# Clustered attention and two gated layers on one core: pair loads behind the mask rows, one set's mask transposed in one go each way, one scratch tile in SBUF

## The chip, the cores and the metric

One program on one core of one Trainium2 chip. The time is device microseconds (us) of one execution, lower is better. Engines: TensorE (PE; its weight loads are PEld), VectorE (DVE), ScalarE (ACT), GpSimd (POOL) and SyncE (SP), which issues nearly all transfers.

## What is computed

From the reference, cut to what matters here:

```python
q_assign = np.argmax(np.einsum('bhsd,hcd->bhsc', q_n, c_n), axis=-1)      # q, k: (2, 8, 768, 64); 16 clusters a head
k_assign = np.argmax(np.einsum('bhsd,hcd->bhsc', k_n, c_n), axis=-1)
mask = q_assign[:, :, :, None] == k_assign[:, :, None, :]
scores = np.where(mask, scale * np.matmul(q, k.transpose(0, 1, 3, 2)), -1000000000.0)
attn = softmax(scores); x = np.matmul(attn, v)                            # then (1536, 512)
h = x @ w_in                                                              # first layer, d_ff 2048
g = (a[0] + a[1] * h + a[2] * h**2 + a[3] * h**3) / (1.0 + np.abs(b[0]) * np.abs(h) + np.abs(b[1]) * h**2 + 1e-06)
x = g @ w_out
# second layer, d_ff 1024: x @ w_in, h * softmax(h), normalised, @ w_out
```

A query attends to the keys of its own cluster only.

## The kernel before

The attention runs over 16 heads of 6 units each (a unit is 128 queries of a head; `units`, index `idx` = 6 n + t for head n and unit t). `unit_scores` makes the scores of a unit in PSUM from four operands: `q1`, `k1` (L398) and `q2`, `k2` (L404). `unit_max` takes the row extreme on DVE (L409), `unit_exp` the exponential on ACT (L422), `turn_p` transposes two units' weights on DVE (L442), and `pv_step` multiplies with the values on PE (L454), one or two heads behind. There are two sets of the four operands, for even and odd heads (`NB = 2`).

The mask sits in 16 extra rows, 64 to 79, of `q2` and `k2`: one row a cluster. They are made for several heads at once. A set (`sets`) is two to four pair tiles `pr` (128 x 768, the q or the k of two heads). Set 0 serves heads 0 and 1, set 1 heads 2 and 3, sets 2, 3 and 4 four heads each. From the pairs PE makes the similarities with the cluster centres (`sims`, L271); ACT copies them out (`keep`, L280); then, for set 1, PE transposes them by token (`by_token`, L284), DVE finds the first maximum (L291 to L305), PE transposes the result back (`mask_t`, L308) and ACT writes it as mask rows `oh1` (`mask_out`, L332). `set1_a` and `set1_b` do this for set 1 in two halves of three tiles each; their PSUM tile is the one that the value products `pv` use afterwards. From `oh` the rows are copied into `q2` and `k2` by two small transfers a head (L374 and L375, 48 KB each), at the end of `prep_head`, which on POOL makes the rest of the next head's operands from the tiles `dup` (loaded by `load_head`, L205 and L206).

All these loads go through SP's one queue, in the order in which they stand there. A tile scheduler fixes that order when the program is built. It hands each transfer the next of eight completion semaphores (`DMAHW0` to `DMAHW7`), so a transfer is issued only after the one eight places ahead of it has landed. The pairs of set k are loaded at unit `AT[k] - LD`, which is unit 17 for set 3 and unit 40 for set 4:

```python
AT = (0, 0, 8, 27, 50)
for k in range(3, len(sets)):
    if idx == AT[k] - LD:
        load_pairs(sets[k])
```

The first layer runs over 48 units too (`ff_units`, a block of 512 tokens by 128 of d_ff). Each has 12 matmuls `h` (L741), a gate on ACT, POOL and DVE (`ff_g1`, `ff_g2`, `ff_g3`, L809 to L831) and 12 matmuls `y` (L848). The gate takes a reciprocal as exp(-ln) and one Newton step; its scratch `r` is the unit's own PSUM tile `hp`. Units 0 and 1 share one PSUM tile of two banks, `h01`. ACT copies the last head's value products out as `u7` and `w7` (L470) behind the first gate's last operation.

Of the kernel before, what the change touches and what calls it, by code (L numbers as in the profile page):

```python
# [7 lines left out]
F32 = mybir.dt.float32  # L8
F32R = mybir.dt.float32r
BF16 = mybir.dt.bfloat16  # L10
# [7 lines left out]
NT = S // 128  # L18
# [12 lines left out]
def fused_kernel(ctx: ExitStack, tc: tile.TileContext, qT, kT, v, cent, w1, w2i, w2o, gln, coef, centT, cst, out):  # L31
    nc = tc.nc
# [17 lines left out]
    def psum4(name):  # L50

        return pvp[0].tile([128, 4, 512], F32, name=name, tag="pv", bufs=1)

    def bank(tag, name):
        return stp.tile([128, 512], F32, name=name, tag=tag)
# [129 lines left out]
    last = {}  # L185

    def load_pairs(es, parts=1):
        for pp, i in es:
            b, p = divmod(pp, 4)
            t = asp.tile([128, S], F32, name=f"pr{pp}{i}", tag="pr", bufs=4)  # L190
            raw["p", pp, i] = t
        w = S // parts
        for c in range(parts):
            for pp, i in es:
                b, p = divmod(pp, 4)
                nc.sync.dma_start(
                    out=raw["p", pp, i][:, w * c:w * c + w],
                    in_=(qT, kT)[i][b, 2 * p:2 * p + 2].rearrange("j d t -> (j d) t")[:, w * c:w * c + w])

    def load_head(n):  # L200
        b, h = divmod(n, H)
        for i, src in enumerate((qT, kT)):
            t = qk.tile([128, S], F32, name=f"dup{n}{i}", tag=f"dup{i}", bufs=2)
            if n:
                nc.sync.dma_start(out=t[0:64], in_=src[b, h])  # L205
            nc.sync.dma_start(out=t[64:128], in_=src[b, h])  # L206
            raw["d", n, i] = t
# [10 lines left out]
    sets = [[(0, 0), (0, 1)], [(1, 0), (1, 1)], [(2, 0), (3, 0), (2, 1), (3, 1)], [(4, 0), (5, 0), (4, 1), (5, 1)], [(6, 0), (7, 0), (6, 1), (7, 1)]]  # L218
# [7 lines left out]
    t = bank("a0", "warm")  # L226
# [22 lines left out]
    mk = {}  # L249
    MS, E, OH = {}, {}, {}  # L250
# [31 lines left out]
    def by_token(k, t, o):  # L282
        M = 32 * len(sets[k])
        return nc.tensor.transpose(o, E[k][0][0:M, t * 128:(t + 1) * 128], ident[0:M, 0:M])  # L284

    def is_max(k, t0, nt, o):
        g = 2 * len(sets[k])
        sv = o.rearrange("p t (g c) -> p t g c", c=C)
        ev = E[k][1][:, t0:t0 + nt].rearrange("p t (g c) -> p t g c", c=C)
        mx = sm.tile([128, nt, g], F32, name=f"mx{k}{t0}", tag=f"mx{nt}{g}", bufs=2)  # L290
        nc.vector.tensor_reduce(mx, sv, axis=AX.X, op=ALU.max)  # L291
        nc.vector.tensor_tensor(ev, sv, mx[:, :, :, None].to_broadcast([128, nt, g, C]), op=ALU.is_equal)

    def rank(k, eng):
        g = 2 * len(sets[k]) * NT
        ev = E[k][1].rearrange("p t (g c) -> p (t g) c", c=C)
        eng.tensor_tensor(ev, ev, rev[:, None, :].to_broadcast([128, g, C]), op=ALU.mult)
# [9 lines left out]
    def mask_t(k, t, o):  # L307
        return nc.tensor.transpose(o, E[k][2][:, t], identb)  # L308
# [20 lines left out]
    def mask_out(k, o, t):  # L329
        masked[k] += o.shape[-1] * (o.shape[1] if len(o.shape) > 2 else 1)  # L330
        M = t.shape[0]
        nc.scalar.activation(out=o, in_=t, func=AF.Identity, scale=MS[k][0:M, 0:1], bias=MS[k][0:M, 1:2])  # L332
# [4 lines left out]
    q2, k1, k2 = [None] * NB, [None] * NB, [None] * NB  # L337
# [8 lines left out]
    def rnd(eng, o, a, scale=1.0):  # L346
        if eng is nc.scalar:
            eng.activation(out=o, in_=a, func=AF.Copy, scale=scale)
            return
        if eng is nc.gpsimd:  # L350
            eng.tensor_scalar(o, a, scale, 0.0, op0=ALU.mult, op1=ALU.add)
        elif isinstance(scale, float) and scale == 1.0:
            eng.tensor_copy(o, a)
        else:
            eng.tensor_scalar(o, a, scale, None, op0=ALU.mult)

    def prep_head(n, er=None, es=None):
        er = er or nc.gpsimd
        es = es or nc.gpsimd
        b, h = divmod(n, H)  # L360
        i = n % NB
        a, c = raw.pop(("d", n, 0)), raw.pop(("d", n, 1))
        rnd(er, k1[i], c, sgn[:, 1:2])
        yield
        es.tensor_tensor(k2[i][0:64], c[0:64], k1[i][0:64].bitcast(F32), op=ALU.subtract)
        yield
        rnd(er, q1[i], a, sgn[:, 0:1])
        rnd(er, q2[i][0:64], a[0:64], -0.125)
        yield
        es.tensor_tensor(q1[i][64:128], a[64:128], q1[i][64:128].bitcast(F32), op=ALU.subtract)  # L370
        yield
        if n:
            assert masked[next(k for k, es in enumerate(sets) if (n // 2, 0) in es)] == S
            nc.sync.dma_start(out=q2[i][64:80].bitcast(F32), in_=mk.pop((n, 0)).bitcast(F32))  # L374
            nc.sync.dma_start(out=k2[i][64:80].bitcast(F32), in_=mk.pop((n, 1)).bitcast(F32))  # L375
        yield


# [201 lines left out]
    M = 32 * len(sets[0])  # L580
# [40 lines left out]
    mp1 = [None]  # L621
# [10 lines left out]

    def set1_a():
        mp1[0] = psum4("set1")
        for a in range(2):
            tp = mp1[0][:, a, 0:3 * M].rearrange("p (t m) -> p t m", t=3)
            for t in range(3):
                by_token(1, 3 * a + t, tp[:, t])
            is_max(1, 3 * a, 3, tp)
        rank(1, nc.vector)  # L640
        first_max(1)

    def set1_b():
        for a in range(2):
            tp = mp1[0][:, 2 + a].bitcast(BF16)
            for t in range(3):
                mask_t(1, 3 * a + t, tp[0:M, t * 128:t * 128 + 128])
            mask_out(1, OH[1][0:M, 384 * a:384 * a + 384], tp[0:M, 0:384])
    load_head(1)
    load_head(2)  # L650
    load_pairs(sets[2])
# [26 lines left out]
    for idx, (n, t) in enumerate(units):  # L678
        if idx == ACL:
            asg.close()  # L680
            wh["r"] = ctx.enter_context(tc.tile_pool(name="wh2", bufs=4, side="right"))
        for k in range(3, len(sets)):
            if idx == AT[k] - LD:
                load_pairs(sets[k])
        if t == 3 and 0 < n < B * H - 2:
            load_head(n + 2)
        if t == 0:
            if n >= 1 and n + 1 < B * H:
                spread(prep_head(n + 1), 7, idx, idx + 6)
        if t == 3:  # L690
            load_v(n)
        sp = unit_scores(n, t)
        m = unit_max(n, t, sp)
        if n == B * H - 1 and t >= NT - 2:
            if t == NT - 2:
                for _ in turn_p(n, NT // 2 - 2):
                    pass
            else:
                end = turn_p(n, NT // 2 - 1)
                next(end)  # L700
        elif t % 2 and idx > 1:
            for _ in turn_p(*divmod(idx // 2 - 1, NT // 2)):
                pass
        if idx == 2:
            with tc.issue_after(last["dve"].ins):
                set1_a()
        if idx == S1B:
            set1_b()
        if idx == 8:
            with tc.issue_after(last["act"].ins):  # L710
                nc.scalar.activation(out=ab, in_=coef_t[:, 4:6], func=AF.Abs)

        m_, i0, i1 = pv_part(n, t)
        if m_ >= 0:
            for i in range(i0, i1):
                pv_step(m_, i)
        if t == 0 and n and n % 2 == 0:
            sums_out(n // 2 - 1, pair_sums(n // 2 - 1), idx + 2)
        unit_exp(n, t, sp, m)
        if n >= 2 and t in (1, 2):  # L720
            pv_out(n - 2, t - 1)
            if t == 2 and n % 2:

                fin_ = pair_fin(n // 2 - 1)
                for i in (1, 2, 3, 4):
                    plan[min(96, idx + i)].append(fin_)
        run_plan(idx)
        if idx == 1:
            set1_0()
# [72 lines left out]
    live = {}  # L802

    def T(tag, u, dt=F32, bufs=1):
        return tmp.tile([128, 512], dt, name=f"{tag}{u}", tag=tag, bufs=bufs)

    def ff_g1(u, hp):
        t, q, y = T("t", u), T("q", u, bufs=2), T("y", u, bufs=3)
        nc.scalar.activation(out=t, in_=hp, func=AF.Abs)  # L809
        last["g"] = nc.scalar.activation(out=y, in_=hp, func=AF.Identity, scale=a3, bias=a2)  # L810
        nc.gpsimd.tensor_scalar(q, t, ab[:, 1:2], ab[:, 0:1], op0=ALU.mult, op1=ALU.add)  # L811
        nc.gpsimd.tensor_tensor(q, q, t, op=ALU.mult)  # L812
        nc.vector.tensor_tensor(y, y, hp, op=ALU.mult)  # L813
        nc.vector.scalar_tensor_tensor(y, y, a1, hp, op0=ALU.add, op1=ALU.mult)
        live[u] = (q, y, hp)

    def ff_g2(u):

# [196 lines left out]
    for u in range(NU + LAG):  # L1015
        if 1 <= u <= NU:
            ff_g2(u - 1)
        if u < NU:
            hp = ff_h(u)
# [77 lines left out]
```

## Time and profile before

| | us |
|---|---|
| median of 3 runs | 661.67 |
| the three runs | 660.16, 661.67, 663.62 |
| the profiled execution: its time | 663.3 |
| its span, first to last instruction | 661.4 |
| PE busy | 602.7 (91%) |
| DVE busy | 493.9 (75%) |
| ACT busy | 443.2 (67%) |
| POOL busy | 386.6 (58%) |

Times in rows are us from the start of the span. A row of an engine's timeline gives start, duration, engine, line, operation and, in brackets, how long the engine was idle before it and what ended that. The busy shares are means over stages with different limits: attention to about 240 us, the first layer to about 500 us, the second layer after it.

### The profile page before, as it was taken

Reading aid. Unit: us, or ns where it says so; the run is one execution under the profiler, and the core shown is the slowest. Engines: PE = TensorE matmul, PEld = TensorE weight load, DVE = VectorE, ACT = ScalarE, POOL = GpSimd, SP = SyncE. Lnnn points to the kernel's source line nnn. Section 1 sums busy time; section 2 is a strip of 40 time slices with the busy share of each in tenths; the row PEclk is TensorE's granted clock in tenths of the full one; section 3 lists DMA queues with packets and bytes.
Section 4 is the critical chain, followed back from the end, with each engine's and each line's share of the span. In section 5 each row is a group of like instructions: output and inputs, shape, how many; then the busy total and the mean of one; then the engine's idle time right before and its main releaser. Section 6 shows DMA issues by size and latency. Waiting matters only on the chain.

```text
span 661.4 us, 13794 instructions
## 1 busy us (share of the span) xinstructions
PE 602.7 (91%) x5517; PEld 469.9 (71%) x5517; DVE 493.9 (75%) x646; ACT 443.2 (67%) x807; POOL 386.6 (58%) x355
## 2 busy tenths in 40 slices
PE   5666897797788889999999999999999999999998
PEld 3444665565556567888888888887788888888887
DVE  4765989989999877897988977779799545444350
ACT  3543676776777778988989879799887434444251
POOL 7741868578679647988998988688977000000000
PEclk8887898999999999999999999999999999999999
DMA  9993558767585242321221322232100000000001
GB/s 214 229 245 100 133 138 238 197 183 190 159 215 134 79 142 94 99 94 63 96 96 64 101 62 92 64 97 64 33 0 1 0 17 17 23 26 16 33 17 48
DMA packets 22440, 64.71 MB, mean 98 GB/s; under 512 B 4533, under 2 KB 5641, under 8 KB 22377
## 3 DMA queue, kind: packets, MB, share of 16 engines
q1 hardware_dynamic: 21944, 63.67, 34.8%
q8 instruction: 43, 0.70, 0.5%
q14 instruction: 21, 0.16, 0.1%
q10 hardware_dynamic: 432, 0.17, 0.1%
HBM read 59.16 MB, written 3.19 MB: 94 GB/s over the span
## 4 chain that ended last, share of the span: by engine, by line
PE 59%; DVE 12%; ACT 8%; issue 3%; POOL 3%; DMA 2%; SPq 1%; ACTq 0%; POOLq 0%; DVEq 0%
PE h L741 17%; PE y L848 17%; PE hh L936 10%; PE o L987 10%; DVE m L409 4%; ACT p L422 3%; DVE pt L442 3%; PE lt L969 2%; PE pv L454 1%; DVE w1f L151 1%; ACT raww L147 1%; PE s L398 1%; DMA rd<-rt 1%; DVE vw L151 1%; DMA rb<-rd 1%
## 5 line engine op out<-in xcount | busy, mean ns | idle before, releaser
L422 ACT ACTIVATE p<-s,m 128x768 f32<-128x768 f32 x96 | 85.9, 897 | 63.6 <-DVE m L409 63.4
L741 PE MATMUL h<-xhl,w1h 128*128 128x512 f32 x336 | 106.4, 392 | 1.7 <-DVE y L825 1.6
L409 DVE TENSOR_REDUCE m<-s 128x1 f32<-128x768 f32 x96 | 88.3, 935 | 22.9 <-PE s L404 22.6
L454 PE MATMUL pv<-pt,v 32*64 32x192 f32 x3072 | 84.3, 338 | 10.2 <-ACT w L470 6.1
L442 DVE STREAM_TRANSPOSE pt<-p 128x1536 f32<-128x1536 f32 (+1 forms) x49 | 84.8, 1730 | 0.2 <-ACT p L422 0.2
L831 POOL TENSOR_TENSOR gl<-y,gh 128x512 fp32r<-128x512 f32 x48 | 71.3, 1489 | 15.5 <-ACT gh L830 15.3
L454 PEld LDWEIGHTS pv<-pt,v 32*64 32x64 f32 x3072 | 57.6, 134 | 31.3 <-issue 17.3
L398 PE MATMUL s<-k,q 128*128 128x384 f32 x192 | 61.0, 401 | 20.4 <-ACT p L422 19.6
L741 PEld LDWEIGHTS h<-xhl,w1h 128*128 128x128 f32 x336 | 62.9, 188 | 16.3 <-DVE y L825 2.4
L848 PE MATMUL y<-gl,w1h 128*128 128x512 f32 x168 | 65.8, 392 | 0.4 <-POOL gl L831 0.4
L812 POOL TENSOR_TENSOR q<-q,t 128x512 f32<-128x512 f32 x48 | 64.4, 1343 | 2.9
L848 PE MATMUL y<-gh,w1l 128*128 128x512 f32 x168 | 65.8, 392 | 0.0
L741 PE MATMUL h<-xhl,w1l 128*128 128x512 f32 x168 | 65.6, 392 | 0.0
L398 PEld LDWEIGHTS s<-k,q 128*128 128x128 f32 x192 | 30.3, 197 | 46.3 <-ACT p L422 27.4
L848 PE MATMUL y<-gh,w1h 128*128 128x512 f32 x168 | 61.7, 392 | 0.0
L404 PE MATMUL s<-k,q 128*128 128x384 f32 x192 | 52.1, 355 | 10.4 <-DMA k<-oh 8.8
L811 POOL TENSOR_SCALAR q<-t,ab 128x512 f32<-128x512 f32 x48 | 42.4, 884 | 26.6 <-ACT t L809 20.6
L813 DVE TENSOR_TENSOR y<-y,h 128x512 f32<-128x512 f32 x48 | 32.8, 684 | 24.7 <-ACT y L810 22.5
L936 PE MATMUL hh<-vh,xhl 128*128 128x512 f32 x160 | 44.9, 396 | 0.0
L404 PEld LDWEIGHTS s<-k,q 128*128 128x128 f32 x192 | 36.8, 199 | 11.1 <-DMA q<-oh 9.0
L823 DVE SCALAR_TENSOR_TENSOR q<-q,h 128x512 f32<-128x512 f32 x48 | 32.7, 682 | 13.5 <-ACT h L821 13.2
L820 ACT ACTIVATE h<-q,qc 128x512 f32<-128x512 f32 x48 | 33.1, 689 | 7.3 <-POOL q L812 4.3
(170 smaller groups left out, 1392.6 us busy)
## 6 DMA issues: line engine op xcount, KB each, us to landing
raww<-in_w SPq DMA_DIRECT2D x32, 512.0 KB, 4.4
v<-in_v SPq DMA_DIRECT2D x64, 192.0 KB, 4.8
dup<-in_qT SPq DMA_DIRECT2D x31, 192.0 KB, 4.1
dup<-in_kT SPq DMA_DIRECT2D x31, 192.0 KB, 4.2
rawv<-in_w2i SPq DMA_DIRECT2D x8, 512.0 KB, 3.7
rawv<-in_w2o SPq DMA_DIRECT2D x8, 512.0 KB, 3.5
out<-ob SPq DMA_DIRECT2D x11, 256.0 KB, 2.0
pr<-in_qT SPq DMA_DIRECT2D x7, 384.0 KB, 7.5
```

The costliest lines, as they stand in the source:

```text
L398: r = nc.tensor.matmul(sp[:, a, 0:384], lhsT=q1[i][:, sl], rhs=k1[i][:, a * 384:(a + 1) * 384], start=True, stop=False)
L404: last["pe"] = nc.tensor.matmul(sp[:, a, 0:384], lhsT=q2[i][:, sl], rhs=k2[i][:, a * 384:(a + 1) * 384], start=False, stop=True)
L409: last["dve"] = nc.vector.tensor_reduce(m, sp[:, :, 0:384], axis=AX.XY, op=ALU.min)
L422: last["act"] = nc.scalar.activation(out=P[n, t // 2][:, t % 2], in_=sp[:, :, 0:384], func=AF.Exp, scale=-1.0, bias=m, accum_out=rs[key][: ...
L442: r = nc.vector.transpose(PT[n][:, 2 * i + m * a:2 * i + m * a + m].rearrange("p t k -> p (t k)"), p[:, m * a:m * a + m].rearrange("p t a ...
L454: last["pv"] = nc.tensor.matmul(pv[n][64 * c:64 * c + 64, r, 0:192].rearrange("p (t q) -> p t q", t=NT), lhsT=vv[n][sl, j], rhs=PT[n][sl, ...
L741: r = nc.tensor.matmul(hp, lhsT=w[:, kt * 128:(kt + 1) * 128], rhs=x[:, kt], start=(i == 0), stop=(i == 11))
L812: nc.gpsimd.tensor_tensor(q, q, t, op=ALU.mult)
L831: nc.gpsimd.tensor_tensor(gl, y, gh.bitcast(F32), op=ALU.subtract)
L848: nc.tensor.matmul(o, lhsT=w[:, c], rhs=g, start=(first and i == 0), stop=(last and i == 2))
L936: last["th"] = nc.tensor.matmul(hp[:, a], lhsT=y[:, kt], rhs=w[:, 512 * a:512 * a + 512], start=(kt == 0 and e == 0), stop=(kt == 3 and e ...
L987: r = nc.tensor.matmul(op[:, 0:m], lhsT=l[:, kt], rhs=w, start=(n == 0), stop=(n == 23))
```

## The change

Three edits. The pair loads of sets 3 and 4 are issued behind the last mask-row transfer that the program has written down by then (`last["mk"]`). Set 1's mask is transposed in one go of six tiles each way, with the maxima and the mask rows behind it. And the first gate (u = 0) gets a tile of its own in SBUF as scratch.

```diff
-            nc.sync.dma_start(out=k2[i][64:80].bitcast(F32), in_=mk.pop((n, 1)).bitcast(F32))
+            last["mk"] = nc.sync.dma_start(out=k2[i][64:80].bitcast(F32), in_=mk.pop((n, 1)).bitcast(F32))
...
     def set1_a():
         mp1[0] = psum4("set1")
+        tp = [mp1[0][:, a, 0:3 * M].rearrange("p (t m) -> p t m", t=3) for a in range(2)]
+        for t in range(NT):
+            by_token(1, t, tp[t // 3][:, t % 3])
         for a in range(2):
-            tp = mp1[0][:, a, 0:3 * M].rearrange("p (t m) -> p t m", t=3)
-            for t in range(3):
-                by_token(1, 3 * a + t, tp[:, t])
-            is_max(1, 3 * a, 3, tp)
+            is_max(1, 3 * a, 3, tp[a])
...
     def set1_b():
+        tp = [mp1[0][:, 2 + a].bitcast(BF16) for a in range(2)]
+        for t in range(NT):
+            mask_t(1, t, tp[t // 3][0:M, t % 3 * 128:t % 3 * 128 + 128])
         for a in range(2):
-            tp = mp1[0][:, 2 + a].bitcast(BF16)
-            for t in range(3):
-                mask_t(1, 3 * a + t, tp[0:M, t * 128:t * 128 + 128])
-            mask_out(1, OH[1][0:M, 384 * a:384 * a + 384], tp[0:M, 0:384])
+            mask_out(1, OH[1][0:M, 384 * a:384 * a + 384], tp[a][0:M, 0:384])
...
             if idx == AT[k] - LD:
-                load_pairs(sets[k])
+                with tc.issue_after(last["mk"].ins):
+                    load_pairs(sets[k])
...
-        live[u] = (q, y, hp)
+        live[u] = (q, y, hp if u else T("r", u))
```

What the scheduler makes of it, at three places. First SP's queue around unit 12, the start of head 2. In the names `dup_630` is head 4's q, `pr_695` to `pr_698` are set 3's pairs, `oh_216` is set 1's mask rows, `q_154` and `k_156` are the operands of even heads (here head 2), `q_160` and `k_162` those of odd heads (head 3). Before:

```order
L206 DMA dup_630<-in_qT 64x768 [waits DMAHW4_49]
L196 DMA pr_695<-in_qT 128x768 [waits DMAHW5_49,PE_49]
L196 DMA pr_696<-in_qT 128x768 [waits DMAHW6_49,PE_49]
L196 DMA pr_697<-in_kT 128x768 [waits DMAHW7_49,PE_49]
L196 DMA pr_698<-in_kT 128x768 [waits DMAHW0_49,PE_49]
L374 DMA q_154<-oh_216 16x768 [waits DMAHW1_49,Activation_49]
L375 DMA k_156<-oh_216 16x768 [waits DMAHW2_49,DVE_49]
L374 DMA q_160<-oh_216 16x768 [waits DMAHW3_49,PE_49]
L375 DMA k_162<-oh_216 16x768 [waits DMAHW4_49]
```

Now:

```order
L206 DMA dup_630<-in_qT 64x768 [waits DMAHW4_49]
L374 DMA q_154<-oh_216 16x768 [waits DMAHW5_49,PE_49,Activation_49]
L375 DMA k_156<-oh_216 16x768 [waits DMAHW6_49,DVE_49]
L374 DMA q_160<-oh_216 16x768 [waits DMAHW7_49,PE_49]
L375 DMA k_162<-oh_216 16x768 [waits DMAHW0_49]
L196 DMA pr_695<-in_qT 128x768 [waits DMAHW1_49]
L196 DMA pr_696<-in_qT 128x768 [waits DMAHW2_49]
L196 DMA pr_697<-in_kT 128x768 [waits DMAHW3_49]
L196 DMA pr_698<-in_kT 128x768 [waits DMAHW4_49]
```

The four row transfers changed places with the four pair loads, which are eight times their size. Further on the same happens with set 4's pairs: they stood ahead of head 6's row transfers and now stand behind head 7's, and head 9's `dup` loads come right after them.

Second PE, from unit 11 (`s_5`, the last of head 1) to unit 12 (`s_0_539`, the first of head 2), as a difference; `pv_451` are head 0's value products, whose PSUM tile is free when `mask_out` has read the second half.

```order
+L454 MATMUL pv_451<-pt_333,v_321 64x192 x32
 L398 MATMUL s_5_505<-k_161,q_159 128x384 x2
 L404 MATMUL s_5_505<-k_162,q_160 128x384 x2
-L454 MATMUL pv_451<-pt_333,v_321 64x192 x56
+L454 MATMUL pv_451<-pt_333,v_321 64x192 x24
 L398 MATMUL s_0_539<-k_155,q_153 128x384 x2
 L404 MATMUL s_0_539<-k_156,q_154 128x384 x2
```

Of 56 value products between the two units, 32 moved ahead of unit 11. On ACT the two `mask_out` now follow each other, and on POOL twelve small operations of set 3 (`scales`) moved ahead of head 3's operands.

Third DVE at the first gate. `h_3314` is the PSUM tile `h01`, `q_3498` and `y_3499` are SBUF tiles, `w1w` and `raww` too. Before:

```order
L151 SCALAR_TENSOR_TENSOR w1w_3514<-w1w_3514,raww_3493 128x512
L823 SCALAR_TENSOR_TENSOR q_3498<-q_3498,h_3314 128x512
L824 SCALAR_TENSOR_TENSOR h_3314<-q_3498,h_3314 128x512
L825 SCALAR_TENSOR_TENSOR y_3499<-y_3499,coef,h_3314 128x512
L519 TENSOR_TENSOR u_3309<-u_3309,w_3310 128x768
```

Now (`r_3506` is the new SBUF tile; lines are one further down):

```order
L151 SCALAR_TENSOR_TENSOR w1w_3515<-w1w_3515,raww_3493 128x512
L824 SCALAR_TENSOR_TENSOR q_3498<-q_3498,r_3506 128x512
L825 SCALAR_TENSOR_TENSOR r_3506<-q_3498,r_3506 128x512
L826 SCALAR_TENSOR_TENSOR y_3499<-y_3499,coef,r_3506 128x512
L519 TENSOR_TENSOR u_3309<-u_3309,w_3310 128x768
```

The order is the same; each of the three operations that had one operand in PSUM has both in SBUF now. Unit 1's matmuls into the other bank of `h01` waited for the last of the three; they now wait for the gate's last read of `h01` (L814 before), which is four DVE operations earlier.

## Rows read from the trace of the kernel before

**Rows 1.** The page's 40 slices: busy tenths of PE, and PE's granted clock.

```profile
PE   5666897797788889999999999999999999999998
...
PEclk8887898999999999999999999999999999999999
```

**Rows 2.** Busy time by stretch: start:end, length, busy (count) by engine, clock, DMA.

```profile
60.00:70.00 10.00, 8.32 (x182) 5.84 (x181) 9.40 (x9) 5.57 (x12) 5.75 (x5) 1.00 0.45 112
...
240.00:430.00 190.00, 187.66 (x1015) 153.25 (x1002) 154.96 (x214) 163.88 (x278) 159.31 (x128) 1.00 0.28 89
430.00:660.00 230.00, 227.13 (x1058) 186.61 (x1057) 136.50 (x226) 127.88 (x236) 67.97 (x55) 1.00 0.09 28
```

**Rows 3.** Waits in 40 to 60 us: who for whom, total, times, longest.

```profile
ACT p L422 <- DVE m L409: 13.8, 2, 11.0
...
PE s L404 <- DMA k<-oh: 8.8, 1, 8.8
```

**Rows 4.** Timeline of PE: units 12 and 13, and a later wait.

```profile
43.52 0.61 PE L398 MATMUL s<-k,q 128*128 128x384 f32 x2
52.89 0.98 PE L404 MATMUL s<-k,q 128*128 128x384 f32 x2 [8.76 <-DMA k<-oh]
53.79 2.22 PE L454 MATMUL pv<-pt,v 32*64 32x192 f32 x48
...
105.75 1.01 PE L398 MATMUL s<-k,q 128*128 128x384 f32 x2 [2.38 <-ACT p L422]
```

**Rows 5.** Timeline of SP's queue: when each transfer was issued.

```profile
42.46 0.80 SPq L196 DMA_DIRECT2D pr<-in_kT  x2
43.35 0.55 SPq L374 DMA_DIRECT2D q<-oh  x1
44.05 0.55 SPq L375 DMA_DIRECT2D k<-oh  x1
...
46.57 0.51 SPq L375 DMA_DIRECT2D k<-oh  x1
...
52.39 0.48 SPq L206 DMA_DIRECT2D dup<-in_qT  x1
```

**Rows 6.** Line 375's transfers (15 in all): issue to landing.

```profile
DMA to landing us min/median/max: 2.1/3.4/6.2
```

**Rows 7.** Busy time by stretch as in rows 2, around unit 12's wait.

```profile
40.00:47.00 7.00, 3.97 (x118) 3.13 (x118) 4.78 (x6) 3.21 (x9) 5.51 (x16) 1.00 1.03 277
47.00:53.00 6.00, 0.11 (x1) 0.14 (x1) 0.00 (x0) 0.00 (x0) 1.84 (x2) 0.53 0.52 127
...
105.00:106.00 1.00, 0.25 (x1) 0.26 (x2) 1.00 (x2) 0.69 (x2) 1.00 (x1) 0.69 1.08 253
```

**Rows 8.** Timeline of DVE: row extreme of unit 13.

```profile
57.63 0.96 DVE L409 TENSOR_REDUCE m<-s 128x1 f32<-128x768 f32 x1 [1.92 <-PE s L404]
```

**Rows 9.** DVE lines 151 and 823: durations in ns, min/median/max.

```profile
L151 DVE SCALAR_TENSOR_TENSOR w1w<-w1w,raww x22: 686/1017/1778, 246.2 to 372.6; 128x512 uint32<-128x512 uint32 x22
...
L823 DVE SCALAR_TENSOR_TENSOR q<-q,h x48: 673/680/690, 248.9 to 509.0; 128x512 f32<-128x512 f32 x48
```

**Rows 10.** Timelines of PE, DVE, ACT and POOL at the first gate.

```profile
248.72 0.88 PE L516 MATMUL rbp<-cst,rw 128*128 128x128 f32 x6
251.20 0.74 PE L741 MATMUL h<-xhl,w1h 128*128 128x512 f32 x2 [1.60 <-DVE y L825]
...
254.08 0.62 PE L741 MATMUL h<-xhl,w1h 128*128 128x512 f32 x2
...
248.94 0.69 DVE L823 SCALAR_TENSOR_TENSOR q<-q,h 128x512 f32<-128x512 f32 x1 [1.00 <-ACT h L821]
...
250.40 0.75 DVE L825 SCALAR_TENSOR_TENSOR y<-y,coef,h 128x512 f32<-128x512 f32 x1
...
252.65 0.81 ACT L470 ACTIVATE w<-pv 64x768 f32<-64x768 f32 x1
...
248.43 2.50 POOL L156 TENSOR_TENSOR w1l<-w1w,w1h 128x512 fp32r<-128x512 f32 x2 [2.10 <-ACT w1h L155]
```

## The prediction

> **What bounds the kernel now.** I began with the page's slices [rows 1]. PE is busy at five to six tenths in the first four slices, to 66 us, and at seven to nine after; its granted clock is lowest, 7, in the fourth, 49.6 to 66.1 us. Next the stages [rows 2]. From 240 us on PE works 187.66 of 190 us and 227.13 of 230: the two layers are PE's, and nothing but a gap in PE shortens them. In an attention stretch such as 60 to 70 us it is DVE that is full, 9.40 of 10 us. So time that is lost in attention comes back only if DVE, PE and ACT all lost it.
>
> The waits show such a place [rows 3]. ACT waits 11.0 us in one go for DVE, PE 8.8 us in one go for a transfer `k<-oh`. The timeline says which unit that is [rows 4]: unit 12, the first of head 2, has its L398 at 43.52 (done at 44.13), but its L404, which reads the mask rows, starts only at 52.89, after 8.76 us of idleness. No engine has other work: in 47 to 53 us PE is busy 0.11 us, DVE and ACT not at all [rows 7].
>
> Why are the rows late? SP issued them at 43.35 and 44.05 [rows 5], so they took about 9 us; the median that the trace gives for line 375 is 3.4 us, its longest 6.2 [rows 6]. The semaphores tell when the transfers ahead landed, since each is issued after the one eight places ahead of it. Head 3's second row transfer (`k_162`), at 46.57, waits for semaphore 4, which is the last `dup` load ahead of the pairs: that had landed by 46.57. The fourth transfer behind it takes semaphore 0 over from the last of the four pairs and goes out at 52.39: that had landed by then [rows 5]. So the pairs held the queue from 46.57 to 52.39, which is 5.82 us, and the rows came right behind them.
>
> **The change, part by part. Set 3's pairs behind the rows.** Eight transfers change places, 8 issues before and 8 after. The rows now follow the `dup` load that landed by 46.57. First way: take the 5.82 us that the pairs held the queue out of the wait. L404 moves from 52.89 to 47.07. Second way, by bytes: four pairs are 4 x 393 KB = 1.57 MB; at the 277 GB/s of 40 to 47 us [rows 7] that is 5.7 us; at the 127 GB/s of 47 to 53 us it would be 12.4 us, more than the whole wait. The gain therefore lies between nothing (if the queue's order is not what holds the rows) and 8.76 us (L404 right behind L398). I take **5.8**, since the landings are the nearest rows. The pairs themselves land some 0.7 us later than before (4 x 49 KB at 277 GB/s); set 3 uses them at unit 27, fifteen units on. What is late next at unit 12 is still the rows: 8.76 - 5.8 leaves a wait of 2.96 us.
>
> **The clock.** In the old wait PE's clock fell to 0.53 on average over 47 to 53 us, and when work came back 48 value products took 2.22 us and DVE waited 1.92 us for unit 13 [rows 4, 7, 8]. If the shorter wait let the clock stand, up to 1.92 us more would come back. But a wait of 2.38 us before 105.75 already let it fall: 0.69 in that microsecond, and an L398 of 1.01 us where it takes 0.61 at full clock [rows 4, 7]. A wait of 2.96 us is longer, so I expect the fall again, and take **0.5** of the 0 to 1.92.
>
> **Set 1's mask in one go.** The same twelve transposes, two maxima and two copies, in another order: nothing is added. 32 of 56 value products go ahead of unit 11 and make it later. The trace counts each as two (24 in the order are the 48 of 2.22 us), so at that low clock 64 would take 2.96 us, at full clock half of it. Unit 12 stands behind all 56 in both orders, so only unit 11's row extreme and exponential come later, and the rest of the wait for the rows hides them. Cost **0**; without that wait up to 3.0. The rows being ready a little earlier gives nothing while the queue decides. POOL's twelve small operations (`scales`) now stand ahead of head 3's operands; they are POOL work in either order, and POOL is busy 5.51 of 7 us before and 1.84 of 6 us in the wait [rows 7], a head ahead of their use: **0**.
>
> **Set 4's pairs behind head 7's rows.** The pairs are loaded ten units before set 4 starts (`LD`), and DMA was 0.45 busy in 60 to 70 us [rows 2], so the queue is not full all the time. Behind them now stand head 9's `dup` loads, which serve POOL a head later. If that cover were gone, they would be late by the pairs' 5.8 us. **0**.
>
> **The first gate's scratch.** PE's gap before unit 1's matmuls, 1.60 us, ends with L825 of the first gate [rows 10]; now they can follow `rbp`, which ends at 248.72 + 0.88 = 249.60. Twelve of them take 254.08 - 251.20 = 2.88 us, so they end at 252.48. But unit 2's go into the PSUM of the last head's products, which ACT frees with `w`, at 252.65 + 0.81 = 253.46, and ACT does this behind the first gate's last copy. So the next wait stands one unit on. With the gate as fast as before, unit 2 starts at 253.5 instead of 254.08: a gain of **0.6** of the 1.6.
>
> Is it as fast? Its three DVE operations now have both operands in SBUF. An operation of this kind with one operand in PSUM, L823, takes 673 to 690 ns in all 48 cases; the one with both in SBUF, L151, of the same size, takes 686 to 1778 ns, 1017 in the median [rows 9]. And POOL works on two-operand subtractions from 248.43 to 250.93 just then [rows 10]. If the three take turns with POOL's two, all five end at about 248.43 + 2.50 + 3 x 0.6 = 252.7, where L825 ended at 250.40 + 0.75 = 251.15: 1.6 later. Then `w` is free at 255.1 and unit 2 starts 1.0 later than before. I take **+1.0** between -0.6 and +1.0 because L151 is the nearer row.
>
> The Trainium skill, page "SBUF — State Buffer", section "Who interferes with whom", speaks against this edit: a DVE instruction with two SBUF inputs shares a read port with GpSimd, and whichever starts second is blocked for the whole instruction of the other. By that rule the sum has +1.0; by L823's duration alone it would have -0.6. The trace agrees as far as L151's spread of 686 to 1778 ns goes; no run yet shows these three operations with both operands in SBUF.
>
> **Sum.** Against the profiled execution's 663.3 (span 661.4 and 1.9 around it): 663.3 - 5.8 - 0.5 + 1.0 = 658.0. That execution lies 1.6 above the median of 661.67, so the median becomes **656.4**.
>
> **The rivals.** *The gate stays fast.* DVE and POOL happen to miss each other, as L151 does in its shortest cases (686 ns): -0.6 instead of +1.0, 654.8. Against it: POOL's two operations are back to back where the three fall.
>
> *The rows come at once.* If the loads ahead of them also run faster without the pairs beside them, the rows are there when L398 ends: 8.76 instead of 5.8, and with no wait there is no fall of the clock (1.92 instead of 0.5): 656.4 - 2.96 - 1.42 = 652.0. For it: 277 GB/s moved just before, for pairs too; against it: the `dup` landing at 46.57 is a measured landing, not a rate.
>
> *The gate's new gap costs the clock.* PE would idle from 252.48 to 255.1, 2.6 us, longer than the 2.38 us that let the clock fall. At half the clock a unit's 2.88 us become 5.76: up to 2.9 more, half of it likely: 657.9, at most 659.3.
>
> *The change doesn't do what it says.* The rows are held by something else (their own path, or all bytes in flight): L404 stays at 52.9, and only the gate remains, 661.67 + 1.0 = 662.7. Against it: the rows landed within half a microsecond of the last pair.
>
> *Slower.* The gate's gap with a whole unit at the low clock costs 1.0 + 2.9 = 3.9 us in the PE-bound layers, where nothing gives it back. It decides from the point where head 2 recovers less than 3.9 us; with nothing recovered the time is 665.6.
>
> **How the numbers follow.** Forecast (655 to 657.5, likeliest 656.4) 0.50; fast gate 0.17; rows at once 0.10; clock at the gate 0.13; rows no sooner 0.07; slower 0.03. What a measurement of this kernel can tell is about 0.5%, 3.3 us: below 658.4 counts as faster. That is the first three and some two thirds of the fourth, 0.86; no change 0.11; slower 0.03. All bounds in the good direction give 656.4 - 2.96 - 1.42 - 1.6 = 650.4, the gate's worst 659.3; the range that leaves out two in ten is 651.5 to 659.5, with the runs' own spread (660.16 to 663.62) in its upper end.
>
> **What would show it.** The pair loads behind four row transfers, and unit 12's L404 near 47.1 instead of 52.89 with a wait of about 3 us before it; PE's clock below full just after; set 3's sims at unit 27 without a wait; DVE's three operations at the first gate longer than 0.7 us in places, `w` later, and PE's gap between units 1 and 2 instead of ahead of unit 1. I am wrong if L404 still waits for the rows till past 50, if the time regained at unit 12 is lost again before 240 us, or if the first layer starts its third unit more than 2 us later against the end of attention.

## The result, and the profile after

| | before | after |
|---|---|---|
| median, 6 runs each on one chip (us) | 661.64 | 655.9 |
| lowest to highest | 660.16 to 663.62 | 655.1 to 656.69 |
| ratio, 95% interval | | 0.9913 [0.9895, 0.9931] |
| the profiled execution: time, span | 663.3, 661.4 | 655.96, 654.2 |

The change makes the kernel 0.9% faster, 5.7 us. The prediction was 656.4. Ratios, here and below, compare undisturbed runs alone, so they aren't always the quotient of the medians. The waits of the changed kernel in 40 to 60 us (who for whom, total, times, longest) answer to [rows 3]:

```profile
ACT p L422 <- DVE m L409: 9.6, 6, 2.4
...
PE s L404 <- DMA k<-oh: 1.4, 1, 1.4
```

Units 12 and 13 on PE's timeline, as [rows 4], and SP's queue, as [rows 5]:

```profile
41.55 0.62 PE L398 MATMUL s<-k,q 128*128 128x384 f32 x2
43.60 0.59 PE L404 MATMUL s<-k,q 128*128 128x384 f32 x2 [1.43 <-DMA k<-oh]
...
45.28 0.62 PE L398 MATMUL s<-k,q 128*128 128x384 f32 x2
```

```profile
37.62 0.54 SPq L374 DMA_DIRECT2D q<-oh  x1
38.77 0.54 SPq L375 DMA_DIRECT2D k<-oh  x1
...
41.97 1.05 SPq L196 DMA_DIRECT2D pr<-in_qT  x2
43.07 0.90 SPq L196 DMA_DIRECT2D pr<-in_kT  x2
```

And by stretch, as [rows 7] (start:end, length, busy by PE, PEld, DVE, ACT, POOL, clock, DMA share, GB/s):

```profile
40.00:47.00 7.00, 5.57 (x139) 3.71 (x137) 6.14 (x7) 2.91 (x7) 6.21 (x5) 1.00 0.63 190
47.00:53.00 6.00, 3.99 (x53) 2.89 (x45) 6.00 (x6) 4.50 (x9) 1.82 (x1) 0.92 1.03 269
53.00:58.00 5.00, 4.84 (x87) 3.04 (x86) 3.04 (x4) 1.89 (x4) 2.17 (x3) 0.75 0.40 97
```

The rows are issued ahead of the pairs, the wait of 8.76 us is 1.43, and 47 to 53 us, empty before, holds 6.00 us of DVE's work. The clock did not fall in the shorter wait (1.00 up to 47 us); it fell some eight microseconds behind it, at about 52 us. L404 starts 9.29 us earlier: 7.33 from the wait and 1.97 because unit 12 itself began earlier, 0.66 of that already at the first unit (14.77 against 15.43).

The first layer's `h` begins at 230.53 instead of 240.43, 9.90 us earlier, but the span ends only 7.2 us earlier. Between them stands the first gate (timelines of DVE, POOL, ACT and PE, as [rows 10]):

```profile
239.09 1.28 DVE L824 SCALAR_TENSOR_TENSOR q<-q,r 128x512 f32<-128x512 f32 x1 [1.03 <-ACT r L822]
240.40 1.67 DVE L825 SCALAR_TENSOR_TENSOR r<-q,r 128x512 f32<-128x512 f32 x1
242.10 0.75 DVE L826 SCALAR_TENSOR_TENSOR y<-y,coef,r 128x512 f32<-128x512 f32 x1
...
238.54 2.98 POOL L156 TENSOR_TENSOR w1l<-w1w,w1h 128x512 fp32r<-128x512 f32 x2 [2.11 <-ACT w1h L155]
...
242.89 0.63 ACT L831 ACTIVATE gh<-y 128x512 fp32r<-128x512 f32 x1 [3.39 <-DVE y L826]
...
244.36 0.80 ACT L470 ACTIVATE w<-pv 64x768 f32<-64x768 f32 x1
...
238.53 0.88 PE L516 MATMUL rbp<-cst,rw 128*128 128x128 f32 x6
239.17 0.70 PE L742 MATMUL h<-xhl,w1h 128*128 128x512 f32 x2
...
245.21 0.73 PE L742 MATMUL h<-xhl,w1h 128*128 128x512 f32 x2 [3.02 <-ACT w L470]
```

```profile
242.00:246.00 4.00, 0.98 (x4) 0.67 (x4) 1.63 (x3) 3.05 (x5) 1.38 (x2) 1.00 0.04 16
246.00:250.00 4.00, 4.00 (x12) 3.11 (x11) 3.18 (x7) 2.07 (x4) 2.08 (x2) 0.58 0.00 0
```

Unit 1 now follows `rbp` at once; PE's gap stands ahead of unit 2 and is 3.02 us long, since `w7` is copied behind the gate's last copy. Behind it the granted clock is 0.58 for 4 us: mostly the lower level, 1.2 GHz.

### The profile page after: what moved, and what is told of

It is laid out like the page before. It is cut to its first block, busy times and chain, and to the rows that moved or that the text cites. A ratio compares the mean times of both kernels' runs of the same rounds, so it can differ in the third digit from the quotient of the medians.

```text
span 654.2 us, 13784 instructions
## 1 busy us (share of the span) xinstructions
PE 601.2 (92%) x5517; PEld 469.7 (72%) x5517; DVE 494.8 (76%) x646; ACT 442.8 (68%) x807; POOL 386.6 (59%) x355
## 4 chain that ended last, share of the span: by engine, by line
PE 64%; DVE 15%; ACT 8%; DMA 5%; POOL 3%; issue 3%; SPq 1%; POOLq 0%; ACTq 0%; DVEq 0%
PE y L849 17%; PE h L742 17%; PE hh L937 10%; PE o L988 10%; DVE m L409 6%; DVE pt L442 4%; ACT p L422 3%; PE pv L454 3%; PE s L398 2%; DMA k<-oh 2%; DMA pr<-in_qT 2%; PE lt L970 2%; PE s L404 2%; POOL u L519 1%; DMA pr<-in_kT 1%
## 5 line engine op out<-in xcount | busy, mean ns | idle before, releaser
L742 PE MATMUL h<-xhl,w1h 128*128 128x512 f32 x336 | 107.8, 397 | 3.1 <-ACT w L470 3.0
L398 PE MATMUL s<-k,q 128*128 128x384 f32 x192 | 61.0, 402 | 20.7 <-ACT p L422 19.9
L398 PEld LDWEIGHTS s<-k,q 128*128 128x128 f32 x192 | 30.4, 198 | 47.0 <-ACT p L422 26.4
L404 PE MATMUL s<-k,q 128*128 128x384 f32 x192 | 51.4, 351 | 2.8 <-DMA k<-oh 2.8
L814 DVE TENSOR_TENSOR y<-y,h 128x512 f32<-128x512 f32 x48 | 32.8, 684 | 25.5 <-ACT y L811 25.1
L831 ACT ACTIVATE gh<-y 128x512 fp32r<-128x512 f32 x48 | 29.9, 631 | 13.3 <-DVE y L826 13.1
L404 PEld LDWEIGHTS s<-k,q 128*128 128x128 f32 x192 | 36.3, 197 | 3.6 <-DMA q<-oh 1.7
```

The costliest lines, as they stand in the source:

```text
L398: r = nc.tensor.matmul(sp[:, a, 0:384], lhsT=q1[i][:, sl], rhs=k1[i][:, a * 384:(a + 1) * 384], start=True, stop=False)
L404: last["pe"] = nc.tensor.matmul(sp[:, a, 0:384], lhsT=q2[i][:, sl], rhs=k2[i][:, a * 384:(a + 1) * 384], start=False, stop=True)
L742: r = nc.tensor.matmul(hp, lhsT=w[:, kt * 128:(kt + 1) * 128], rhs=x[:, kt], start=(i == 0), stop=(i == 11))
```

## The experiments

In each group the kernels ran on one chip with the kernel before. Single executions of one kernel spread over 5 to 15 us, so most readings below are from the traces.

**One edit at a time.** Pairs alone (`e1_pairs`), set 1 alone (`e2_set1`), the gate alone (`e3_gate`), and the first two without the gate (`e4_no_gate`). The edits are those of the diff above; of the third:

```diff
-        live[u] = (q, y, hp if u else T("r", u))
+        live[u] = (q, y, hp)
```

> The first edit alone: the pairs of sets 3 and 4 issued behind the mask rows; set 1's two halves and the first gate as before. Theory (the pair loads held the rows; that is where the gain comes from): the wait for k<-oh ahead of unit 12's L404 falls from 8.76 us to 1 to 3 us, and without the gate's cost the time is 2 to 3 us below that of the changed kernel: 652.5 to 654. Rival (set 1's mask in one go makes the rows themselves ready sooner, and that is what took the wait away): the wait stays above 5 us and the time is 657 to 661. Part of the changed kernel's gain up to unit 12 was 1.97 us that unit 12 itself started earlier; if that came from set 1's order it is missing here (654.5).

> The second edit alone: set 1's mask transposed in one go each way; pairs and gate as before. Theory (its order is worth nothing while the pairs hold the queue): L404 of unit 12 still starts near 52.9 us, the wait is 8 to 10.5 us, and the time is 661 to 662, the same as before. Rival (it brings the rows sooner): L404 starts at 50 us or earlier, and the time is 657 to 659.

> The third edit alone: the first gate's scratch in SBUF. Theory (the three VectorE operations with both operands in SBUF take turns with GpSimd's two, PE's gap moves on to unit 2 and its clock falls there): L824 and L825 take over 1.2 us each, PE waits about 3 us ahead of unit 2, the clock in the 4 us behind it is below 0.8, and the time is 663.5 to 664.5. Rival (the gate costs what the sum had, 1.0, and the clock fell for another reason): 662 to 663 with a clock above 0.9 there. Rival (it gains): 661.

> The first two edits without the third: the first gate's scratch is back in PSUM. Theory (the third edit costs 2.6 us, 9.9 us gained up to the end of attention against 7.2 at the end of the span): 653 to 653.5. Rival (the third edit costs the 1.0 of the sum and the rest was lost elsewhere): 654.5 to 655. Rival (it gives 0.6): 656.5.

| | median (before 663.49) | ratio, 95% interval |
|---|---|---|
| e1_pairs | 657.8 | 0.9899 [0.9865, 0.9934] |
| e2_set1 | 658.9 | 0.9916 [0.988, 0.9951] |
| e3_gate | 664.75 | 1.0021 [0.9992, 1.0049] |
| e4_no_gate | 657.33 | 0.9894 [0.9854, 0.9933] |

The pairs alone carry the gain, and the order of set 1 adds nothing to it that can be told (0.9899 and 0.9894, each with an interval of about 0.4% on either side). Against their own before both gain 6 us by the medians, 7 by the ratios, not the 8 that I expected without the gate: the 2.6 us that I put on the gate came from one execution, in which the clock had fallen. `e3_gate` reads in its trace as its theory had it (operations of 1.27 and 1.67 us, a gap of 2.50 ahead of unit 2, a clock of 0.73 in the 3 us behind), but its time, 0.2% up, is not told from no change. The miss is `e2_set1`: expected to be like before, it gains almost as much alone. Its SP queue shows what differs:

```profile
35.64 0.81 SPq L196 DMA_DIRECT2D pr<-in_qT  x2
38.17 0.55 SPq L374 DMA_DIRECT2D q<-oh  x1
38.81 0.55 SPq L375 DMA_DIRECT2D k<-oh  x1
39.45 1.01 SPq L196 DMA_DIRECT2D pr<-in_kT  x2
```

With set 1's operations in another order the scheduler put head 2's rows between the pairs: two ahead of them, not four. So the two edits don't add up; the second does by accident half of what the first does by intent (unit 12 also began 2.2 us earlier in this profile, 1.2 of it already at the first unit). It also gives a count of pairs against the rows' time:

| | pairs ahead | `k<-oh` issued | L404 starts | from issue | PE's wait |
|---|---|---|---|---|---|
| before | 4 | 44.05 | 52.89 | 8.8 | 8.76 |
| e3_gate | 4 | 40.41 | 49.39 | 9.0 | 6.45 |
| e2_set1 | 2 | 38.81 | 44.74 | 5.9 | 2.83 |
| after | 0 | 38.77 | 43.60 | 4.8 | 1.43 |
| e4_no_gate | 0 | 42.07 | 46.64 | 4.6 | 1.41 |
| e1_pairs | 0 | 40.08 | 43.22 | at most 3.1 | none |

From four pairs to two the rows' time falls by 1.5 us a pair. What the last two cost can't be told: with none ahead the profiles of the groups below took 4.3 us (`e4_again`), 4.7 (`e7_wait`) and 7.2 (`e6_no_clash`), the last more than `e2_set1` with two. `e3_gate`, which has before's attention, waited 6.45 us: the 8.76 of [rows 4] was a long case.

`e1_pairs` had no wait for the rows at all, and yet its profiled execution took 661.16 us. It lost its gain later, at places where it has the same work as the changed kernel. From unit 45's row extreme to unit 48's it needed 9.48 us (123.69 to 133.17), the changed kernel 7.21 (120.44 to 127.65). Here is that stretch in windows of 3 us that begin at the same place of the work, `e1_pairs`:

```profile
118.00:121.00 3.00, 1.36 (x36) 0.76 (x34) 3.00 (x4) 2.68 (x5) 1.83 (x2) 1.00 0.34 93
121.00:124.00 3.00, 2.53 (x24) 1.73 (x32) 3.00 (x4) 2.94 (x5) 0.47 (x1) 0.73 0.64 179
124.00:127.00 3.00, 3.00 (x52) 1.93 (x44) 2.67 (x3) 1.57 (x5) 2.92 (x3) 0.50 1.05 232
```

and the changed kernel:

```profile
114.75:117.75 3.00, 1.35 (x36) 0.76 (x34) 3.00 (x4) 2.68 (x5) 1.84 (x2) 1.00 0.61 178
117.75:120.75 3.00, 2.32 (x34) 1.76 (x40) 3.00 (x4) 2.94 (x5) 0.46 (x1) 1.00 0.66 174
120.75:123.75 3.00, 2.89 (x61) 1.87 (x42) 3.00 (x3) 1.56 (x5) 2.92 (x3) 1.00 1.06 236
```

PE had done the same 36 matmuls in the first window, 1.36 and 1.35 us of work; behind it the clock went to 0.50 in the one and stayed at 1.00 in the other. Of all twelve profiles of this document three fell at this place (9.48 to 9.59 us between the two row extremes), nine did not (7.20 to 7.23). So which of the light places costs a fall differs from one execution to the next, at 2.3 us a fall here, and much of the runs' spread goes with it: over the 26 runs of the kernel before in this group the time falls with the mean granted clock (correlation -0.89), from 666 to 667 us at 0.966 and 0.967 to 658 to 661 at 0.981 and 0.982.

**The gate, beside the kernel without it.** `after_again` is the changed kernel, `e4_again` the one without the third edit; `e5_uw_first` orders the last head's copies ahead of the first gate's last copy on ACT; `e6_no_clash` was to hold GpSimd's two subtractions back (`held` keeps them until there). First the edit of `e5_uw_first` (`last["out"]` is the last L470), then that of `e6_no_clash`:

```diff
+    last["w7"] = last["out"]
...
-        nc.scalar.activation(out=gh, in_=y, func=AF.Copy)
+        r = nc.scalar.activation(out=gh, in_=y, func=AF.Copy)
+        if u == 0:
+            behind(r, last["w7"])
```

```diff
-        nc.vector.scalar_tensor_tensor(y, y, a0, r, op0=ALU.add, op1=ALU.mult)
+        e = nc.vector.scalar_tensor_tensor(y, y, a0, r, op0=ALU.add, op1=ALU.mult)
+        if u == 0:
+            for l, w, h in held:
+                behind(nc.gpsimd.tensor_tensor(l, w, h.bitcast(F32), op=ALU.subtract), e)
```

> The changed kernel once more, on the same chip as the three runs beside it. Theory (the third edit costs about 1 us by the operations that take turns, and up to 1.75 us more where PE's clock falls in the first gate, which it also did in two of the four profiles that had the scratch in PSUM): 0.990 to 0.993 of the time before, 1 to 2 us above the run without the third edit. Rival (the third edit costs nothing that can be measured): the same time as without it. From the start of the bias product rbp to the end of the span it takes 415.2 to 415.7 us where the clock falls, as in both profiles so far.

> The first two edits without the third, once more, beside the changed kernel. Theory: 1 to 2 us below the changed kernel; from rbp to the end 412.7 to 413.0 us where PE's clock stays up in the first gate, 414.5 where it falls. Rival (the third edit costs nothing): the same time.

> The changed kernel with the last head's copies u7 and w7 ordered ahead of the first gate's last copy on ScalarE. Theory (PE's 3.02 us ahead of unit 2 are the wait for w7, which stood behind the gate's last copy, and the clock falls in that gap): the gap is gone, unit 2 follows unit 1, the clock stays up, and from rbp to the end it takes 410.5 to 411.5 us: 4 to 5 us below the changed kernel. Rival (something else holds unit 2, or the next unit waits instead): 414 us or more.

> The changed kernel with GpSimd's two subtractions w1l of that moment ordered behind the last VectorE operation of the first gate. Theory (VectorE's two long operations, 1.28 and 1.67 us, are long because GpSimd works beside them): all three take 0.69 to 0.75 us, y is ready 1.5 us sooner, PE's gap ahead of unit 2 is 1.4 to 1.6 us instead of 3.0, and from rbp to the end it takes 414.0 us with a fall of the clock, 412.3 without. Rival (both operands in SBUF are slow by themselves): the operations stay above 1.2 us and the gap at 3.0.

| | median (before 662.68) | ratio, 95% interval |
|---|---|---|
| after_again | 656.51 | 0.9936 [0.9901, 0.9971] |
| e4_again | 654.33 | 0.9879 [0.9827, 0.993] |
| e5_uw_first | 654.52 | 0.9882 [0.9828, 0.9936] |
| e6_no_clash | 657.8 | 0.9942 [0.9907, 0.9976] |

The medians have the third edit 2.2 us to the bad, but the intervals overlap. `e6_no_clash` tells nothing of its question: its edit sets an order without a wait, and between two engines that held nothing back: GpSimd started its subtractions at 240.32 beside DVE's 240.87 as ever, and the operations took 1.27 and 1.67 us. In `e5_uw_first` `w7` is copied at 240.47, ahead of `gh`, and PE has no gap: it works 3.00 us in every 3 from 238 to 256 us. By the medians it is 2.0 us below the changed kernel, not the 4 to 5 that I expected; from `rbp` to the end of the span it took 411.5 us, as expected. ACT's timeline:

```profile
240.47 0.81 ACT L470 ACTIVATE w<-pv 64x768 f32<-64x768 f32 x1
243.01 0.63 ACT L832 ACTIVATE gh<-y 128x512 fp32r<-128x512 f32 x1 [1.74 <-DVE y L827]
```

**GpSimd held back with a wait, and head 4's loads behind the rows.** `e7_wait` is `e6_no_clash` with a dependency that makes a semaphore wait (`DependencyClass.Sync`) in the place of `behind`. `e8_dups` is `e5_uw_first` with one more group of loads moved:

```diff
         if t == 3 and 0 < n < B * H - 2:
-            load_head(n + 2)
+            with tc.issue_after(last["mk"].ins) if n == 2 else ExitStack():
+                load_head(n + 2)
```

> The changed kernel with GpSimd's two subtractions w1l made to wait for the last VectorE operation of the first gate; the run before this one only set an order among instructions recorded and GpSimd didn't wait, so it told nothing apart. Theory (they are long because GpSimd works beside them): the two operations of 1.28 and 1.67 us take 0.69 to 0.75 each, PE's gap ahead of unit 2 is 1.4 to 1.7 us instead of 3.0 to 3.3, and from rbp to the end it takes 412.9 us where the clock stays up (414.4 with the clash), 414 to 414.5 where it falls. Rival (both operands in SBUF are slow by themselves): they stay above 1.2 us, the gap stays at 3.0.

> The kernel with the last head's copies first (e5_uw_first), and head 4's dup loads issued behind head 2's mask rows too. Theory (the rest of the wait ahead of unit 12's L404, 0 to 3.3 us from one execution to the next, is the dup loads in front of the rows): no wait for k<-oh at unit 12, the rows land in 2 to 3.5 us from their issue, and the time is that of e5_uw_first or up to 1.5 us less: 0.986 to 0.989 of the time before. Rival (the dups are needed sooner than they look): GpSimd's operands of head 4 come later and a wait shows at unit 24 of 1 us or more.

| | median (before 662.26) | ratio, 95% interval |
|---|---|---|
| e7_wait | 652.34 | 0.9858 [0.9807, 0.9909] |
| e8_dups | 651.01 | 0.9828 [0.978, 0.9875] |

In `e7_wait` GpSimd waits, and the operations are short (DVE, POOL, PE; lines are five further down):

```profile
236.70 0.69 DVE L829 SCALAR_TENSOR_TENSOR q<-q,r 128x512 f32<-128x512 f32 x1 [1.03 <-ACT r L827]
237.43 0.69 DVE L830 SCALAR_TENSOR_TENSOR r<-q,r 128x512 f32<-128x512 f32 x1
238.16 0.75 DVE L831 SCALAR_TENSOR_TENSOR y<-y,coef,r 128x512 f32<-128x512 f32 x1
...
239.05 2.51 POOL L834 TENSOR_TENSOR w1l<-w1w,w1h 128x512 fp32r<-128x512 f32 x2 [5.00 <-DVE y L831]
...
241.27 0.73 PE L747 MATMUL h<-xhl,w1h 128*128 128x512 f32 x2 [1.49 <-ACT w L475]
```

All three have their operands where the changed kernel has them; only GpSimd is missing beside them. So operands in SBUF are not slow by themselves. Nor is GpSimd beside them enough: before, with one operand in PSUM, L823 took 0.69 beside the same subtractions, and these 2.50 [rows 10]. It takes both, and GpSimd pays too (2.98 against 2.51 for its two). The changed kernel's two subtractions one by one (durations in ns min/median/max, first and last start in us) show how:

```profile
L156 POOL TENSOR_TENSOR w1l<-w1w,w1h x1: 1282/1282/1282, 238.5 to 238.5; 128x512 fp32r<-128x512 f32 x1
L156 POOL TENSOR_TENSOR w1l<-w1w,w1h x1: 1739/1739/1739, 239.8 to 239.8; 128x512 fp32r<-128x512 f32 x1
```

The first began alone and took the 1.28 us that it takes without DVE; DVE's first operation, which began 0.55 us into it, ended 0.55 us behind it (240.37). The second subtraction ended 1.15 us behind that (241.52), and DVE's second operation 0.55 us behind that (242.07). So the engines took turns by whole operations. `e8_dups` has no wait for the rows at unit 12 (L404 at 41.98, 3.7 us after the issue at 38.25); the `q<-oh` ahead of it landed 2.3 us after its issue. Unit 12 was 1.2 us ahead of `e5_uw_first`, but by the end of head 2 that was gone: the clock was 0.50 in 52 to 54 us, where `e5_uw_first` had 1.00. No wait at unit 24 shows. The two spans are 650.1 and 650.2, so its median, lower than expected (0.9828, not 0.986 to 0.989), isn't shown to be the loads' doing.

Put together, what the first gate costs, from the start of `rbp` to the end of the span, where PE is all that counts:

| | scratch | idle ahead of unit 1 or 2 | clock behind it | `rbp` to end |
|---|---|---|---|---|
| before; e2_set1; e4_again | PSUM | 1.60; 1.90; 1.91 | stays up | 412.7; 413.0; 413.1 |
| e1_pairs; e4_no_gate | PSUM | 1.89; 1.90 | falls | 414.5; 414.6 |
| after_again | SBUF | 3.28 | stays up | 414.4 |
| e3_gate; e6_no_clash; after | SBUF | 2.50; 2.76; 3.02 | falls | 415.2; 415.4; 415.7 |
| e7_wait (no clash) | SBUF | 1.49 | stays up | 412.7 |
| e5_uw_first; e8_dups | SBUF | none | stays up | 411.5; 411.4 |

Counted from the layer's first `h` instead, the same profiles lie closer: with the clock up 421.0 to 421.1 us with the scratch in PSUM and 422.2 in SBUF, with a fall 422.5 to 422.6 and 423.7 to 423.8. By that the edit costs 1.1 to 1.3 us and a fall 1.4 to 1.7; `e7_wait` took 420.7, `e5_uw_first` and `e8_dups` 419.5 and 419.4.

## Why the prediction came out, point by point

**Set 3's pairs (5.8): right in mechanism, slightly small.** The rows stood behind the pairs in the queue, as the 5.82 us between the two issues had it, each of which waited for a landing. The longest of 6.2 us in [rows 6] leaves the row in question out, since the trace gives no landing for it; line 374's (min/median/max), with the row just ahead of it as the longest, bears out the 9 us:

```profile
DMA to landing us min/median/max: 3.2/5.5/9.2
```

The profiled pair gave 7.33, but before's wait was a long one: the two profiles with four pairs ahead waited 7.6 us on average, the eight with none ahead (all but `e8_dups`, which moves more) 0 to 3.33 and 1.2 on average. That is 6.4. So the rest of the wait, 2.96 us in the sum, was too long for seven of the eight, and in three of them (`e1_pairs`, `after_again`, `e5_uw_first`) the rows were there in time, as that rival had it. What was left points to the four `dup` loads that still stood ahead of the rows: in seven of the eight the first of these loads was still on its way when the second row was issued, and the row landed 1.8 to 3.1 us behind it (in the changed kernel at 41.19 and 43.46, in `e6_no_clash`, the longest wait, at 41.05 and 44.18). In `e1_pairs` it had landed before and the row took 2.1 us, and in `e8_dups`, without these loads ahead, the row that has a landing took 2.3. Set 3's similarities waited for no pair, as forecast.

**The clock at unit 12 (0.5): not to be read from a wait's length.** I argued from 2.38 us at 105.75 to 2.96. Here 1.43 us left the clock up and it fell eight microseconds later; behind the 2.83 us of `e2_set1` it fell (the next L398 took 1.01), behind the 3.33 us of `e6_no_clash` it did not (a matmul of 0.60, and 0.51 for the next). In these profiles it is no function of the wait's length, so the term belongs in the range, not in the sum.

**Set 1 in one go (0): right beside the first edit, wrong alone.** "The rows being ready a little earlier gives nothing while the queue decides" held for the work on the engines; but the edit moves the queue itself, as `e2_set1` shows. The order printed for both edits at once could not show this.

**Set 4's pairs (0): right.** Between the row extremes of units 36 and 94 the changed kernel loses 0.16 us against before: 111.44 and 101.44 at unit 36, 236.03 and 226.19 at unit 94.

**The first gate's scratch (+1.0): right in mechanism, small by what follows.** The gap moved to unit 2, `w7` came behind the gate's last copy, and the first two of DVE's three operations took turns with GpSimd's two: 239.09 to 242.85 is 3.76 us where 248.94 to 251.15 was 2.21, 1.55 more against the 1.6 of the sum. With the clock up the edit costs 1.3 to 1.7 us (414.4 against 412.7 to 413.1), with a fall on both sides 0.6 to 1.2; from the first `h`, 1.1 to 1.3 in both cases, near the sum's 1.0. What the sum left out is the fall itself, which was put down as a rival: it costs 0.8 to 1.9 from `rbp`, 1.4 to 1.7 from the first `h`, and came in three of four profiles with the long gap, in two of six with one of 1.49 to 1.91. So the rival of the gate's new gap, given 13 in 100, was what the changed kernel's profile showed, without deciding the time. The rival of a gate that stays fast fell: all six profiles of this gate with GpSimd beside it have 1.27 or 1.28 and 1.67 or 1.68 us. By the Trainium skill, page "SBUF — State Buffer", section "Who interferes with whom", a VectorE instruction with two SBUF inputs and a GpSimd instruction that reads SBUF contend for a shared pair of ports, which whoever is first holds for its whole instruction while the other is blocked. The trace agrees: DVE's 1.28 and 1.67 us each end 0.55 us behind a subtraction, GpSimd's second 1.15 us behind DVE's first, and with GpSimd held back (`e7_wait`) DVE's two take 0.69.

**The sum** came out in part by luck: the stall's 0.6 more lies against the gate's 0.3 to 2 more, and what the clock's falls add differs from one execution to the next. The rivals of rows no sooner and of a slower kernel fell with `e1_pairs`.

## What to carry to other kernels

A small transfer that an engine is waiting for belongs ahead of large ones in a queue, and the queue's order has to be read after every edit, also one that touches no transfer. Moving a wait was worth nothing here until what stands behind it on the other engine moved too: the third edit cost 1.3 to 1.7 us as it stood, and with `u7` and `w7` ahead of `gh` it took 1.2 to 1.6 us off the first gate (411.5 against 412.7 to 413.1). With a spread of 5 to 15 us and effects of 1 or 2, stretches of the trace between two fixed points (from `rbp` or the first `h` to the end) told what medians could not.

## What the runs showed of the hardware

The granted clock fell to its lower level (1.2 GHz) behind some light stretches of PE and not behind others with the same work (1.36 and 1.35 us busy of 3), and executions differ by where it fell: by 2.3 us at the place between units 45 and 48, by 1.4 to 1.7 at the first gate. A VectorE operation with both operands in SBUF took 0.69 us alone and 1.27 to 1.68 beside GpSimd's subtractions, which took 2.98 us instead of 2.51 for two: each waited for the other's operation to end. With one operand in PSUM neither lost time (0.69 and 2.50). Mask rows of 48 KB landed up to 9.2 us after their issue with four pair loads ahead, and 2.1 us after it in `e1_pairs`, with none.
